# An unused early read on SyncE, and a small VectorE step placed behind a later copy

## The chip, the cores and the metric

The kernel runs on one core of a Trainium2 chip. The metric is device time in microseconds (us) of one execution, the median of several runs. Engines are named as in the profile: PE is TensorE (PEld its weight loads), DVE is VectorE, ACT is ScalarE, POOL is GpSimd, SP is SyncE.

## The reference

Two layers in a row. The first is a linear recurrence over 768 time steps for 4 batches and 8 heads of width 64, whose state decays by a constant per head; the second is a feed-forward layer over the 3072 resulting tokens of width 512, with 2048 hidden units and a "snake" activation:

```python
for t in range(S):
    state = gamma[None, :, None, None] * state + np.einsum('bhd,bhe->bhde', k[:, :, t], v[:, :, t])
    y[:, :, t] = scale * np.einsum('bhd,bhde->bhe', q[:, :, t], state)
...
h = x @ w_in
s = np.sin(alpha * h)
g = h + s * s / (alpha + 1e-09)
return (g @ w_out).astype(np.float32)
```

`alpha` has one value for each hidden unit, so `1 / (alpha + 1e-9)` is 2048 numbers: a tile `rec_alpha` of 128 partitions by 16.

## The kernel before

The recurrence is worked in chunks of 128 time steps. The 24 chunks (4 batches of 6) stand in a list `order`: the first chunk of each batch, called `e0` to `e3`, come first, since they need no state. They are grouped by 4, 2, 2, ..., 4 into the groups `g` of the feed-forward layer. For a chunk, q and k are transposed on TensorE (`half_T`, `stage_T`, copies at L292 to L307), the scores are formed (`stage_A`) and masked with the decay on VectorE (`mask_A`, tile `aT`, L345), and multiplied by v (`stage_M`, L371), whose result is copied into `xT` (L374), the input of the feed-forward layer.

A `Slot` is one step of the first feed-forward matrix: four matmuls into `ph` (L558, weights from `w_in`), the sine on ScalarE (L561, scaled by `alpha_sb`), a square on ScalarE or VectorE (`sq`, L566 or L568), and `add` on VectorE (L573), `gT = s * rec_alpha + ph`. The output matmuls with `w_out` are `ff_out` (L583, `po`); `pairs(f)` issues two of them.

The order of the instructions on every engine is written by hand: each engine works through its own list in the order of the statements and waits by semaphores for the others. The stage that the change touches is the first 25 us. There

- SyncE issues the loads `near` of q and k of chunk `e0` (L160), then `alpha_row` (L163), and nothing more until the first output at 43.8 us;
- GpSimd issues all other loads as DMAs of its own (L95, L119, L150, L154), in the order in which they are written, from the ninth on each behind the landing of the one eight places ahead of it, and works `decay_table(3)` (L254) between two of them;
- TensorE transposes `alpha_row` into PSUM (L703), ScalarE copies it to `alpha_sb` (L712), and VectorE forms `rec_alpha` from it (L728 and L729). Its first reader is the first `add`, that of slot "a";
- VectorE's list around it reads: mask of `e2`, `rec_alpha` (two instructions), copy of `stage_M(e2)` into `xT` (L374), copy of `half_T(e3, 0)` (L294), `scale_v(e2)` (L175), square of slot "a" (L568), then `add` of slots "a" and "b", the mask of `e3`, `add` of slot "c";
- `idle_work` puts matmuls on a tile of zeros between TensorE's first steps; their result is not used.

Of the kernel before, what the change touches and what calls it, by code (L numbers as in the profile page):

```python
# [8 lines left out]
F32 = mybir.dt.float32  # L9
# [7 lines left out]
def kernel(  # L17
# [15 lines left out]
    nc = tc.nc  # L33
# [22 lines left out]
    consts = ctx.enter_context(tc.tile_pool(name="consts", bufs=1))  # L56
# [9 lines left out]
    w_in_v = moe_w_in.rearrange("(ko ki) f -> ki ko f", ki=128)  # L66
# [3 lines left out]
    def half(x):  # L70
        return slice(64 * x, 64 * x + 64)
# [10 lines left out]
    def chunk_of(t, j):  # L82
        b, c = divmod(j, NCH)
        return t[b, :, c * C:(c + 1) * C, :].rearrange("h s d -> s h d")
# [12 lines left out]
    def by_rows(j, name):  # L97
        return name == "q" and j in order[1:4] or name == "k" and j in order[2:4]
# [59 lines left out]
    for name, src in (("q", q), ("k", k)):  # L158
        near[name] = work.tile([128, d_model], F32, name="o_sb", tag="o_sb", bufs=3).rearrange("i (h d) -> i h d", h=H)
        nc.sync.dma_start(out=near[name], in_=chunk_of(src, 0))  # L160
        raw[name, 0] = big.tile([128, H, D], BF16, name=f"{name}b")
    alpha_row = consts.tile([FF, 128], F32, name="alpha_row")
    nc.sync.dma_start(out=alpha_row, in_=moe_alpha.rearrange("(fo fi) -> fo fi", fi=128))  # L163

# [93 lines left out]
    alpha_sb = consts.tile([128, FF], F32, name="alpha_sb")  # L258
    rec_alpha = consts.tile([128, FF], F32, name="rec_alpha")
# [9 lines left out]
    def half_T(j, i, eng, bank=None):  # L269

        if i == 0:
            if j in order[2:4]:
                st["qkT", j] = big.tile([128, 2 * NP, 128], BF16, name="qkT0", tag="qkT0", bufs=2)
                st["kT", j] = st["qkT", j][:, NP:]
            else:
                st["qkT", j] = work.tile([128, 2 * NP, 128], BF16, name="qkT", tag="qkT", bufs=6)
        pt = psum.tile([128, NP, 128], BF16, name="pr" if by_rows(j, "qk"[i]) else "pt", tag="mm",
                       bufs=4) if bank is None else bank.rearrange("i (p t) -> i p t", p=NP)
        o = st["qkT", j][:, i * NP:(i + 1) * NP, :]
        if by_rows(j, "qk"[i]):  # L280
            for f in range(8):
                for x in range(2):
                    nc.tensor.transpose(pt.rearrange("i p t -> i (p t)")[half(x), 64 * f:64 * f + 64],
                                        raw["qk"[i], j][half(x), f, :], ident[half(x), half(x)])
            o = o.rearrange("d m (i f) -> d m i f", f=8)
            pt = pt.rearrange("d p t -> d (p t)").rearrange("d (f m i) -> d m i f", f=8, m=NP)
        else:
            for m in range(NP):
                for x in range(2):
                    nc.tensor.transpose(pt[half(x), m, :], raw["qk"[i], j][:, 4 * x + m, :], ident)  # L290
        if eng is nc.scalar:
            nc.scalar.copy(o, pt)  # L292
        else:
            nc.vector.tensor_copy(o, pt)  # L294
# [331 lines left out]
    def idle_work(n):  # L626
        for _ in range(n):
            nc.tensor.matmul(spare["ps"], warm[:, :128], warm, start=True, stop=True)  # L628
# [42 lines left out]
    def slot(name, f, lo, hi, nf=1, tag="mm"):  # L671
        sl[name] = Slot(0, f, (lo, hi), nf, tag)
# [52 lines left out]
    mask_A(e2)  # L725
    nc.scalar.activation(out=kgq, in_=expoq, func=ACTF.Exp, scale=-1.0)
    idle_work(2)
    nc.vector.tensor_scalar_add(rec_alpha, alpha_sb, 1e-9)  # L728
    nc.vector.reciprocal(rec_alpha, rec_alpha)  # L729
    nc.scalar.activation(out=tiny, in_=warm[:, 0:1], func=ACTF.Sin)  # L730
    load_chunk(order[4], "q")
    decay_table(3)
# [18 lines left out]
    stage_M(e2, front[:, 0], nc.vector)  # L751
    idle_work(1)
    half_T(e3, 0, nc.vector)
    half_T(e3, 1, nc.scalar)
    slot("a", 0, 0, n3, 1, "mm")
    scale_v(e2, nc.vector)
# [201 lines left out]
```

## Time and profile before

| | |
|---|---|
| runs | 210.97, 211.01, 212.22 us; median 211.01 |
| the profiled execution | 210.62 us, of which the span from its first to its last instruction is 208.8 |
| busy, of the span | PE 97%, DVE 75%, ACT 73%, POOL 55% |
| matmuls L558 and L583 | 98.1 and 94.8 us busy |
| first `ph` matmul | at 16.39 us |
| `rec_alpha` | add at 13.88 us for 1.62 us, reciprocal at 15.54 us for 0.25 us |
| `alpha_row` | issued on SP at 1.88 us, lands 3.8 us later |

Times in the profile are in us from the start of the span, unless a column says ns. A line of a timeline gives the start, the duration, the engine, the source line, the operation, the tiles written and read, and in brackets how long the engine stood idle before it and what ended that. The chain of waits follows the work that ended last back through whatever released it. In the DMA view a queue's line gives packets, megabytes and the share of the time of 16 DMA engines that its packets took; q1 is the queue of SyncE, q0 that of GpSimd.

### The profile page before, as it was taken

The numbers are of one execution on the slowest core, as the hardware profiler recorded it, in microseconds if no ns is written. First come the engines' busy times: TensorE is split into PE (matmuls) and PEld (weight loads), VectorE is DVE, ScalarE is ACT, GpSimd is POOL, SyncE is SP. The second block draws the span as 40 slices with busy tenths as digits, with TensorE's granted clock in tenths as the row PEclk, the third lists the DMA queues.
The fourth block names the chain that finished last, engine by engine and source line by source line (L and its number), as shares of the span: only waits on it lengthen the run. The fifth ranks groups of instructions, "written<-read, shape, count | busy, mean of one in ns | idle before, by whom it ended". The sixth has DMA issues, their size and how long they took to land.

```text
span 208.8 us, 5979 instructions
## 1 busy us (share of the span) xinstructions
PE 202.4 (97%) x2473; PEld 124.2 (59%) x2473; DVE 156.1 (75%) x322; ACT 151.5 (73%) x309; POOL 115.0 (55%) x155
## 2 busy tenths in 40 slices
PE   7798999999999999999999999999999999999994
PEld 2354544457776666666666766766767664444453
DVE  5799897797989978868878868869788965656220
ACT  7667598748997787687687687686785779999001
POOL 8996469999998989899499901002022200000000
PEclk9999999999999999999999999999999999999999
DMA  8999999999999999999999992412412101010212
GB/s 126 167 192 196 194 193 181 167 189 170 161 163 103 151 108 203 170 74 196 117 178 128 180 156 56 104 57 46 102 56 50 52 3 52 0 50 3 100 50 100
DMA packets 98187, 24.78 MB, mean 119 GB/s; under 512 B 88544, under 2 KB 95216, under 8 KB 98160
## 3 DMA queue, kind: packets, MB, share of 16 engines
q0 software_dynamic: 75408, 13.38, 85.8%
q1 hardware_dynamic: 22608, 10.96, 24.8%
q8 instruction: 19, 0.31, 0.7%
q14 instruction: 8, 0.07, 0.1%
q10 hardware_dynamic: 144, 0.07, 0.1%
HBM read 27.27 MB, written 6.29 MB: 161 GB/s over the span
## 4 chain that ended last, share of the span: by engine, by line
PE 90%; DVE 4%; DMA 2%; POOL 1%; issue 1%; ACT 0%; POOLq 0%; DVEq 0%; ACTq 0%
PE ph L558 39%; PE po L583 39%; DMA qf<-in_q_dram 2%; PE py L396 2%; DVE aT L345 2%; PE poh L608 2%; PE py L450 1%; PE pt L303 1%; PE pa L406 1%; DVE gT L573 1%; DVE rec_alpha L728 1%; PE py L459 1%; PE pa L413 1%; PE pa L435 1%; PE spare L628 1%; POOL k L119 1%
## 5 line engine op out<-in xcount | busy, mean ns | idle before, releaser
L573 DVE SCALAR_TENSOR_TENSOR gT<-s,rec_alpha,ph 128x256 bf16<-128x256 f32 (+3 forms) x164 | 79.7, 522 | 31.6 <-ACT s L566 31.4
L558 PE MATMUL ph<-xT,w_in 128*128 128x256 bf16 (+3 forms) x656 | 98.1, 291 | 0.8 <-DVE xT L374 0.8
L561 ACT ACTIVATE s<-ph,alpha_sb 128x256 f32<-128x256 f32 (+3 forms) x164 | 76.0, 506 | 30.3 <-PE ph L558 30.2
L583 PE MATMUL po<-w_out,gT 128*128 128x512 bf16 x368 | 94.8, 380 | 0.1
L558 PEld LDWEIGHTS <-w_in 128*128 128x128 bf16 x656 | 63.3, 98 | 33.7 <-issue 0.9
L566 ACT ACTIVATE s<-s 128x512 f32<-128x512 f32 (+1 forms) x91 | 56.9, 626 | 2.8
L583 PEld LDWEIGHTS <-gT 128*128 128x128 bf16 x368 | 34.0, 98 | 30.2 <-DVE gT L573 0.8
L529 POOL CAST s_q<-s_f 128x256 bf16<-128x256 f32 x5 | 2.0, 396 | 34.9 <-DVE s_f L514 18.4
L595 DVE COPY o_sb<-po 128x512 f32<-128x512 f32 x20 | 13.8, 689 | 9.9 <-PE po L583 9.8
L139 POOL DMA_DIRECT2D qk_seq<-in_q_dram x24 | 16.9, 745 | 4.0 <-DMA v_seq<-in_v_dram 3.9
L139 POOL DMA_DIRECT2D qk_seq<-in_k_dram x24 | 16.9, 748 | 1.4 <-DMA qk_seq<-in_q_dram 1.4
L139 POOL DMA_DIRECT2D v_seq<-in_v_dram x24 | 16.8, 756 | 0.0
L175 POOL TENSOR_TENSOR v_seq<-v_seq,kgq 128x512 bf16<-128x512 bf16 x13 | 13.5, 1063 | 5.1 <-DMA v_seq<-in_v_dram 5.1
L503 DVE TENSOR_TENSOR xT<-py,qg 128x512 bf16<-128x512 f32 x19 | 13.0, 682 | 0.4 <-PE py L466 0.4
L421 DVE TENSOR_TENSOR aTw<-pa,maskq 128x768 bf16<-128x768 f32 x13 | 12.3, 949 | 0.0
L119 POOL DMA_DIRECT2D vr<-in_v_dram x11 | 10.3, 944 | 0.4 <-DMA w_out<-in_moe_w_out_dram 0.3
L628 PE MATMUL spare<-warm 128*128 128x512 bf16 x24 | 8.6, 467 | 1.2 <-DVE warm L196 1.2
L612 ACT COPY o_sb<-poh 128x256 f32<-128x256 f32 (+1 forms) x2 | 0.6, 318 | 11.7 <-PE poh L608 11.2
L409 DVE TENSOR_TENSOR aT<-pa,mask 128x1024 bf16<-128x1024 f32 x7 | 8.5, 1219 | 0.0
L150 POOL DMA_DIRECT2D w_in<-in_moe_w_in_dram x7 | 5.6, 811 | 1.6 <-DMA w_out<-in_moe_w_out_dram 1.6
L529 ACT CAST s_q<-s_f 128x256 bf16<-128x256 f32 x14 | 5.5, 391 | 1.1 <-DVE s_f L525 0.6
L396 PE MATMUL py<-qkT,s_q 64*64 64x128 bf16 x160 | 6.1, 228 | 0.0
(113 smaller groups left out, 169.8 us busy)
## 6 DMA issues: line engine op xcount, KB each, us to landing
out_dram<-o_sb SPq DMA_DIRECT2D x23, 256.0 KB, 2.7
w_in<-in_moe_w_in_dram POOLq DMA_DIRECT2D x6, 256.0 KB, 11.0
w_out<-in_moe_w_out_dram POOLq DMA_DIRECT2D x3, 512.0 KB, 11.5
vr<-in_v_dram POOLq DMA_DIRECT2D x11, 128.0 KB, 6.3
qk_seq<-in_q_dram POOLq DMA_DIRECT2D x16, 80.0 KB, 6.8
qk_seq<-in_k_dram POOLq DMA_DIRECT2D x16, 80.0 KB, 5.3
v_seq<-in_v_dram POOLq DMA_DIRECT2D x16, 80.0 KB, 6.0
w_out<-in_moe_w_out_dram POOLq DMA_DIRECT2D x2, 256.0 KB, 7.1
```

What stands on the lines that cost most here:

```text
L119: nc.gpsimd.dma_start(out=t, in_=chunk_of(src, j))
L139: nc.gpsimd.dma_start(out=o, in_=src[bt, head(b, m, e), cs[0] * C:, :].rearrange("(f i) d -> i f d", i=64))
L175: eng.tensor_mul(t, t, by[:, j % NCH, :, None].to_broadcast([128, H, D]))
L421: return {"mask": lambda: nc.vector.tensor_mul(aT, pa[:, :, 0:384].rearrange("p e (m t) -> p e m t", m=2), maskq[:, None, None, :].to_broa ...
L503: nc.vector.tensor_mul(o, st["pyw", old][:, :, 0:256].rearrange("p b (m t) -> p b m t", m=2), by)
L558: nc.tensor.matmul(self.ph[:, m, :], w_in[:, i, f * 128:(f + 1) * 128], xT[g][:, i, self.lo:self.hi], start=(m == 0 and i == 0), stop=(i = ...
L561: nc.scalar.activation(out=self.s[:, m, :], in_=self.ph[:, m, :], func=ACTF.Sin, scale=alpha_sb[:, f:f + 1])
L566: nc.scalar.activation(out=self.s, in_=self.s, func=ACTF.Square)
L573: nc.vector.scalar_tensor_tensor(gT[self.g][:, f, self.lo:self.hi], self.s[:, m, :], rec_alpha[:, f:f + 1], self.ph[:, m, :], op0=ALU.mult ...
L583: nc.tensor.matmul(po[g, ts], gT[g][:, f, ts * C:(ts + 1) * C], w_out[:, f, :], start=(f == 0), stop=(f == FF - 1))
L595: nc.vector.tensor_copy(o_sb, po[g, ts])
L628: nc.tensor.matmul(spare["ps"], warm[:, :128], warm, start=True, stop=True)
```

## The change

It has two parts. After the `near` loads, SyncE issues one more DMA, which reads 32 rows of 256 float32 (1 KB each) of `w_in` into a tile `wake` that nothing reads; `alpha_row` follows it. And the two instructions of `rec_alpha` are issued behind VectorE's copy of `half_T(e3, 0)`, instead of ahead of the copy of `stage_M(e2)`.

```diff
@@ -159,6 +159,8 @@
         nc.sync.dma_start(out=near[name], in_=chunk_of(src, 0))
         raw[name, 0] = big.tile([128, H, D], BF16, name=f"{name}b")
+    wake = consts.tile([32, 256], F32, name="wake")
+    nc.sync.dma_start(out=wake, in_=w_in_v[0:32, 0, 0:256])
     alpha_row = consts.tile([FF, 128], F32, name="alpha_row")
@@ -725,8 +727,6 @@
     idle_work(2)
-    nc.vector.tensor_scalar_add(rec_alpha, alpha_sb, 1e-9)
-    nc.vector.reciprocal(rec_alpha, rec_alpha)
     nc.scalar.activation(out=tiny, in_=warm[:, 0:1], func=ACTF.Sin)
@@ -751,6 +751,8 @@
     stage_M(e2, front[:, 0], nc.vector)
     idle_work(1)
     half_T(e3, 0, nc.vector)
+    nc.vector.tensor_scalar_add(rec_alpha, alpha_sb, 1e-9)
+    nc.vector.reciprocal(rec_alpha, rec_alpha)
     half_T(e3, 1, nc.scalar)
```

No other instruction changes its place on any engine.

## The prediction

> **What bounds the kernel now.** I read the page first, then the chain of waits from 7 to 24 us, then the timeline of VectorE and GpSimd there, then the DMA view. The page (first line: span; then busy time and chain by engine):
>
> ```profile
> span 208.8 us, 5979 instructions
> PE 202.4 (97%) x2473; PEld 124.2 (59%) x2473; DVE 156.1 (75%) x322; ACT 151.5 (73%) x309; POOL 115.0 (55%) x155
> PE 90%; DVE 4%; DMA 2%; POOL 1%; issue 1%; ACT 0%; POOLq 0%; DVEq 0%; ACTq 0%
> ```
>
> TensorE is 90% of the chain. From 22 us on it is busy nearly without a break, so whatever is won must be won before it, by starting that row of matmuls earlier. The chain of waits there (start, length, what):
>
> ```profile
> 3.09 4.83 DMA qf<-in_q_dram
> 7.97 0.44 PE pr L283 x16
> ...
> 12.75 1.22 DVE aT L345
> 13.97 1.55 DVE rec_alpha L728
> ...
> 15.71 0.64 DVE xT L374
> ...
> 16.39 0.82 PE ph L558 x4
> ...
> 19.67 1.13 DVE aT L345
> 20.80 0.53 DVE gT L573
> ...
> 21.38 0.82 PE po L583 x3
> ```
>
> Both places of the change lie near it. `rec_alpha`'s add stands on it for 1.55 us, ahead of the copy `xT` (L374) for which the first `ph` matmul waits 0.78 us. The load `qf` stands on it because `pr` waits 0.38 us for it; the new read runs just before that.
>
> **Why the add takes 1.62 us.** It handles 16 numbers per partition. The timeline (start, length, engine, line):
>
> ```profile
> 13.88 1.62 DVE L728 TENSOR_SCALAR rec_alpha<-alpha_sb 128x16 f32<-128x16 f32 x1
> 14.32 1.14 POOL L254 TENSOR_TENSOR qg<-qg,step 128x512 f32<-128x512 f32 x1
> 15.32 0.85 POOL L150 DMA_DIRECT2D w_in<-in_moe_w_in_dram  x1
> 16.12 0.79 POOL L150 DMA_DIRECT2D w_in<-in_moe_w_in_dram  x1
> 16.25 0.68 DVE L294 COPY qkT<-pr 128x512 bf16<-128x512 bf16 x1
> 17.91 0.56 DVE L568 TENSOR_TENSOR s<-s 128x384 f32<-128x384 f32 x1 [0.39 <-ACT s L561]
> ```
>
> It ends at 15.50, GpSimd's multiply at 15.46. So it looks held until GpSimd is done, after which it needs about 0.04 us. Two casts from and to SBUF show the same against GpSimd's DMA issues:
>
> ```profile
> 3.98 0.56 DVE L689 CAST qb<-o_sb 128x512 bf16<-128x512 f32 x1 [0.28 <-DMA o_sb<-in_q_dram]
> 4.24 0.63 POOL L95 DMA_DIRECT2D qf<-in_q_dram  x1
> 5.29 0.75 DVE L693 CAST kb<-o_sb 128x512 bf16<-128x512 f32 x1 [0.75 <-DMA o_sb<-in_k_dram]
> 5.73 0.95 POOL L119 DMA_DIRECT2D vr<-in_v_dram  x1
> ```
>
> They end at 4.54 and 6.04, 0.30 and 0.31 us after one issue gives way to the next, although their lengths differ by 0.19 us. So a held cast gets in where one DMA issue follows another. The Trainium skill, SBUF — State Buffer, section Who interferes with whom, says that GpSimd and a VectorE copy or scalar operation of this kind share a port pair by an exclusive lock, held for a whole instruction; by that rule, the trace agrees (15.50 against 15.46).
>
> **The move, step by step.** Removed at its old place: 1.55 us of chain for the add, and 0.25 us from 15.46 to the start of `xT` at 15.71 for its end and the reciprocal. Without them `xT` waits only for its matmuls (L371, 14.25 to 14.66): about 14.71 to 15.35. The copy of `half_T(e3,0)` needs `pr`, which ends at 15.36: 15.40 to 16.08. Nothing else moves on VectorE. TensorE issues the second `pr` group until 15.61 in any case, so the first `ph` starts at 15.61 instead of 16.39: at most 0.78 us is won. ScalarE is free for the first sine (its table load ends 15.55, its copy of `pr` 16.25): 16.53 instead of 17.30.
>
> Added at the new place: the same two instructions, between that copy and `scale_v(e2)` (L175, 0.68 us), which stands ahead of the first square (L568). Instructions on VectorE start some 0.09 us before the previous one's end, so the add asks at about 15.99. GpSimd has no gap from 1.38 to 16.91, so its hours do not move with VectorE: its first `w_in` issue gives way at 16.12, its second ends at 16.91, and then it waits for a landing until 17.70. Two outcomes:
> - It gets in at 16.12: `scale_v` starts 0.25 us later, 16.37, ends 17.05, before the sine ends (17.12). The square starts at 17.14 instead of 17.91. The whole 0.77 us remains.
> - It misses and is held to 16.91: `scale_v` 17.16 to 17.84, square at about 17.8 instead of 17.91. About 0.1 us remains, as everything behind (gT, the mask `aT` of e3, gT, then `po`) is a row of VectorE work.
>
> So the move is worth 0.1 to 0.77 us. What waits behind the add if it is held: `scale_v(e2)`, the square, and TensorE's `po`, which had next to no spare time (0.27 us of waiting at 21.38).
>
> **The read `wake`, step by step.** 32 KB on SyncE between the `near` loads and `alpha_row`. Nothing reads it, so no engine waits for it. SyncE: one issue more (L160 0.57 us, L163 0.82), so `alpha_row` is issued at about 2.5 to 2.7 instead of 1.88 and lands, at its 3.8 us, near 6.5; its transpose runs at 8.68, so 2 us cover it. SyncE's next work is at 43.8 us. The DMA engines: packets of 1 KB show in the stretch 6.0 to 6.4 us:
>
> ```profile
> DMA packets 70, 0.07 MB, mean 179 GB/s; under 512 B 0, under 2 KB 70, under 8 KB 70
> q0 software_dynamic: 70, 0.07, 112.7%
> ```
>
> That is 1.127 x 16 x 0.4 us / 70 = 0.103 us of an engine each. Two per engine, if the 32 spread evenly over 16, are 0.21 us, or 0.18 at the 1.13 packets that overlap. The engines are full then, so `qf` lands between 0 and 0.2 us later; I take 0.1, as they need not run ahead of the packets of `qf`. The Trainium skill, DMA: Bandwidth & Descriptors, section Queues, rings and completion order, lets each engine take turns between its queues packet by packet; by that rule the read does delay `qf`, and the sum would be its upper end, 0.2; no row here separates these. The delay moves VectorE's row from 8 us on, and with it the add's request: 15.99 + 0.1 = 16.09, just ahead of 16.12; at 0.2 it is 16.19, and the gap is missed.
>
> **What is given back.** Landings do not come earlier. `w_in`'s second piece is issued at 9.57 and lands 7.8 us later, 17.37, used at 18.11; the piece for slot 8 is issued at 15.32, lands 11.6 later, 26.92, and its weights are loaded at 27.48. Spare time is 0.74 and 0.56 us, less the 0.1 by which the read puts loads off. So of 0.77 - 0.1 = 0.67 us TensorE keeps about 0.45. Later landings have over 1 us (w_out's last, 28.56 + 10.5 = 39.06, used 40.10).
>
> **Sum.** -0.67 + 0.22 = -0.45 us. The profiled execution took 210.62 us, span 208.8 and 1.8 around it; the runs' median is 211.01, 0.4 above, for the same program. Against the median: 210.6. That is 0.2%; a measurement of this kernel tells about 1% from no change.
>
> **Rivals.**
> 1. The stall moves. The add misses the gap and waits to 16.91: gain 0.1, 210.9 us. For it: the request and the gap lie 0.03 us apart in my sum. Against: the two casts each got in at the next gap.
> 2. Slower: the 1.55 us are the instruction's own (its first use, or its source), not GpSimd's. Then the add runs 15.99 to 17.61, `scale_v` 17.86 to 18.54, the square at 18.46 instead of 17.91: +0.55, 211.6 us. It decides as soon as the add ends after 17.1 at its new place. For it: L207, another small one of these, took 0.54 us. Against: that one too ends (2.45) where a GpSimd issue ends (2.48), and the agreement at 15.46.
> 3. The read costs more. Its bound: `o_sb` of k, 1024 packets, landed in 4.0 us, 64 per engine, 0.06 us for 256 B, so up to 0.25 for 1 KB and 0.5 for two. Even so, held to 16.91, the gain is 0.1 to 0; 211.0 us.
> 4. The read helps the loads behind it. In 1.6 to 2.4 us the engines moved 232 packets, in 2.4 to 3.2 already 864: a slow start. If it shortened `qf`'s 4.83 us, `pr` could come 0.38 earlier: with the move 0.38 + 0.77 = 1.15 us, 209.9. Against: those first packets are the `near` loads, which the read follows.
> 5. The change does nothing: another wait (the second `pr` group, sine, landings) holds TensorE at today's hours: 211.0 us.
>
> **Chances.** Forecast 0.38, rival 1 0.22, rival 2 0.12, rival 3 0.05, rival 4 0.08, rival 5 0.05; 0.10 for what no row shows. All worked-out cases lie within 1% of 211.01 (208.9 to 213.1). The three runs themselves differ by 0.6%, and the starting state of the loads can move an early stage more than I see; this puts 0.16 below and 0.12 above, 0.72 within. Range 209.4 to 212.0: from rival 4 less the runs' own scatter to rival 2 plus it.
>
> **What would show it.** Right: the add at its new place under 0.3 us, ending by 16.2; first `ph` near 15.7; the square near 17.2; `po` (three) near 20.8 instead of 21.38. Stall moved: the add ends at about 16.95. Rival 2: 1.6 us there whatever GpSimd does. For the read: `qf` lands after 7.92, `alpha_row` stays off the chain. Wrong altogether: TensorE waiting for a landing before 30 us by over 0.5 us, or a span beyond 207.3 to 210.

## The result, and the profile after

| | before | after |
|---|---|---|
| median of the runs made side by side | 211.88 us (20 runs) | 210.61 us (20 runs) |
| profiled execution, and its span | 210.62, 208.8 us | 210.65, 208.9 us |

The ratio is 0.9964 with a 95% interval of 0.9946 to 0.9981, so the change makes the kernel faster by 0.36%, or 0.76 us (0.40 to 1.14). The comparison leaves disturbed executions out, so this is not the ratio of the two medians. The two profiled executions are equal, and the profile shows why. The page of after:

```profile
span 208.9 us, 5981 instructions
PE 202.3 (97%) x2473; PEld 124.1 (59%) x2473; DVE 154.4 (74%) x322; ACT 151.6 (73%) x309; POOL 115.1 (55%) x155
PE 92%; DMA 3%; DVE 2%; POOL 1%; issue 0%; ACT 0%; POOLq 0%; ACTq 0%
```

VectorE is busy 1.7 us less, and its share of the chain fell from 4% to 2%. Lines from L163 on carry higher numbers than before: L558 is now L560, the add is L754. The chain of waits of after (start, length, what):

```profile
3.09 5.76 DMA qf<-in_q_dram
8.90 0.44 PE pr L285 x16
...
15.92 0.62 PE pr L285 x32
16.54 0.77 PE ph L560 x4
...
18.01 0.57 DVE s L570
...
21.48 0.82 PE po L585 x3
```

`rec_alpha` has left the chain: the first `ph` now follows TensorE's own second `pr` group. But `qf` took 5.76 us instead of 4.83, so `pr` starts 0.93 us later than before (8.90 against 7.97). At `ph` the lag is 0.15 us by the chain and at `po` 0.10: this execution lost 0.93 us at a landing and won it back behind it. The timeline of VectorE and GpSimd in after shows the add at its new place:

```profile
16.94 0.20 DVE L754 TENSOR_SCALAR rec_alpha<-alpha_sb 128x16 f32<-128x16 f32 x1
16.35 1.55 POOL L150 DMA_DIRECT2D w_in<-in_moe_w_in_dram  x2
17.15 0.75 POOL L150 DMA_DIRECT2D w_in<-in_moe_w_in_dram  x1
```

The second POOL line is the second of the two issues in the line above it. The add takes 0.20 us instead of 1.62 and ends at 17.14, where one issue gives way to the next: the same gap that the prediction aimed at, 1.03 us later. GpSimd's row came later too, 0.46 us of it in a wait for a landing of `w_in` ahead of 13.54 us that before did not have.

For the experiments I read one more number from each trace: by how much a certain matmul starts later than the same matmul of the profiled before. It is called the lag, at `pr` (8.05 us in before), at a `ph` at 19.26, at a `po` at 37.35 and at the last `poh` at 205.60. For after it is +0.93, +0.10, +0.10, +0.10.

### The profile page after: what moved, and what is told of

Same layout as the page of the kernel before. It is cut to its first block, busy times and chain, and to the rows that moved or that the text cites. A ratio compares the mean times of both kernels' runs of the same rounds, so it can differ in the third digit from the quotient of the medians.

```text
span 208.9 us, 5981 instructions
## 1 busy us (share of the span) xinstructions
PE 202.3 (97%) x2473; PEld 124.1 (59%) x2473; DVE 154.4 (74%) x322; ACT 151.6 (73%) x309; POOL 115.1 (55%) x155
## 4 chain that ended last, share of the span: by engine, by line
PE 92%; DMA 3%; DVE 2%; POOL 1%; issue 0%; ACT 0%; POOLq 0%; ACTq 0%
PE ph L560 39%; PE po L585 39%; DMA qf<-in_q_dram 3%; PE py L398 2%; PE poh L610 2%; PE py L452 1%; PE spare L630 1%; DVE aT L347 1%; PE pt L305 1%; PE pa L408 1%; DVE gT L575 1%; PE py L461 1%; PE pa L415 1%; PE pa L437 1%; PE front L373 1%; POOL k L119 1%
## 5 line engine op out<-in xcount | busy, mean ns | idle before, releaser
L560 PE MATMUL ph<-xT,w_in 128*128 128x256 bf16 (+3 forms) x656 | 98.1, 291 | 0.0
L560 PEld LDWEIGHTS <-w_in 128*128 128x128 bf16 x656 | 63.2, 98 | 33.0 <-issue 0.2
L347 DVE TENSOR_TENSOR aT<-pa,dec 128x1024 bf16<-128x1024 f32 x4 | 4.9, 1219 | 1.8 <-PE pa L335 1.8
```

The costliest lines, as they stand in the source:

```text
L560: nc.tensor.matmul(self.ph[:, m, :], w_in[:, i, f * 128:(f + 1) * 128], xT[g][:, i, self.lo:self.hi], start=(m == 0 and i == 0), stop=(i = ...
```

## The experiments

Each run was timed beside the kernel before on its own chip; ratios are to that kernel, in brackets the 95% interval.

### The two parts, alone and together

`neither` is the kernel before once more and `both` the changed kernel once more. `move` has only this:

```diff
-    nc.vector.tensor_scalar_add(rec_alpha, alpha_sb, 1e-9)
-    nc.vector.reciprocal(rec_alpha, rec_alpha)
...
     half_T(e3, 0, nc.vector)
+    nc.vector.tensor_scalar_add(rec_alpha, alpha_sb, 1e-9)
+    nc.vector.reciprocal(rec_alpha, rec_alpha)
```

and `read` only this:

```diff
+    wake = consts.tile([32, 256], F32, name="wake")
+    nc.sync.dma_start(out=wake, in_=w_in_v[0:32, 0, 0:256])
```

> The kernel before once more, as a measure of how far its own front varies. Both theories: ratio 1.000 within 0.002. If the 0.93 us by which qf landed later in the changed kernel's profile (8.85 us against 7.92) is a matter of the execution, qf lands here somewhere between 7.9 and 8.9; if the read causes it, it lands near 7.9 again. The rec_alpha add takes about 1.6 us at its old place.

> rec_alpha at its new place, no read. Theory A (the move pays, the read costs): 0.5 to 0.8 us faster than before, ratio 0.9962 to 0.9976, at least as fast as both parts together; the add takes 0.2 to 0.3 us at its new place, qf lands near 7.9. Theory B (the read pays by making the start steadier, the move is neutral): ratio 0.999 to 1.001.

> The read of w_in, rec_alpha at its old place. Theory A: 0.1 to 0.9 us slower than before, ratio 1.0005 to 1.004, and the rec_alpha add again held about 1.6 us until GpSimd's multiply ends; qf lands later than 7.92. Theory B: ratio near 0.9964 as with both parts, with fewer runs near 212 us.

> The changed kernel once more, on the same chip as its two halves. Both theories: ratio about 0.996. If the late qf landing belongs to the read, it lands near 8.85 again; if to the execution, anywhere between 7.9 and 8.9.

| | ratio | median us | lag at pr, ph, po, end | the add |
|---|---|---|---|---|
| neither | 1.0014 [0.9978, 1.0050] | 211.82 | +1.14, +0.69, +1.74, +1.74 | 0.71 us |
| move | 0.9964 [0.9922, 1.0005] | 210.97 | +0.41, -0.42, -0.01, -0.02 | 0.19 us |
| read | 1.0024 [0.9980, 1.0068] | 211.77 | +0.14, +0.14, +0.30, +0.29 | 1.61 us |
| both | 0.9988 [0.9941, 1.0034] | 211.14 | +0.61, -0.21, +1.23, +1.30 | 0.17 us |

What follows. The move alone comes out at the 0.9964 of the whole change, though its own interval just reaches past 1; the read alone gives no gain. The changed kernel once more, `both`, comes out at 0.9988, with 0.9964 inside its interval. From `pr` to `ph`, after, move and both each win 0.83 us, to the hundredth, whatever their `pr` lost; read, with the add at the old place, wins nothing there. `neither` shows the lottery in the old place: its front ran later (the `near` load of k took 4.80 us instead of 4.0, and the lag is 1.52 from 8.8 us on), GpSimd's list had come further when the add asked, and the add was held 0.71 instead of 1.62 us; its lag also falls by 0.83, to 0.69. So 0.83 us is all that can be won there, because TensorE's second `pr` group then sets the first `ph`; the move makes sure of it.

Behind `ph`, however, `neither` loses 1.05 us, `both` 1.44 and `move` 0.41, by 37 us. The groups of the trace put it on single squares of VectorE. The timeline of both:

```profile
28.05 2.18 DVE L570 TENSOR_TENSOR s<-s 128x512 f32<-128x512 f32 x1
28.61 1.06 POOL L256 TENSOR_TENSOR qg<-qg,step 128x512 f32<-128x512 f32 x1
```

A square of this size takes 0.68 us at 26.66, just ahead of it; this one takes 2.18 and ends at 30.23, 0.56 us after GpSimd's multiply ends (29.67). In neither one took 1.78 us at 28.95; in move one took 1.58 us at 32.00 and also ended 0.56 us after a multiply. In before the four squares between 26 and 35 us take 0.68 to 0.85 us; the longest also ends 0.56 us after a multiply, which it met only at its tail. The multiplies are `decay_table(1)`, `(4)` and `(2)`, which stand behind DMA issues that wait for landings, so that their hours shift from execution to execution and meet a square or don't. The next runs take this away.

### Another source for the add, and earlier tables

`psum` leaves the add at its old place but lets it read the PSUM tile `pal`, from which ScalarE copies `alpha_sb`:

```diff
-    nc.vector.tensor_scalar_add(rec_alpha, alpha_sb, 1e-9)
+    nc.vector.tensor_scalar_add(rec_alpha, pal, 1e-9)
```

`tables` works the three decay tables right behind `load_w_out(2)`, at 18.5 to 21.5 us, between VectorE's first square (17.2 us) and its next (26.2 us):

```diff
     load_w_out(2)
+    for c in (1, 4, 2):
+        decay_table(c)
...
-    decay_table(1)
...
-    decay_table(4)
...
-    decay_table(2)
```

`move_tables` and `psum_tables` join the latter to `move` and to `psum`. None of the four has the read.

> rec_alpha at its old place and no read, but the add takes alpha from the transpose's PSUM tile instead of alpha_sb. If GpSimd holds the add because it takes both operands' sides from SBUF (theory H), the add takes 0.2 us at about 14.0 and xT follows when its matmuls are done, so the row behind it comes as early as with the move (0.8 us earlier than with the add held), ratio 0.9955 to 0.998. If the wait belongs to the place or to the instruction itself (rival), it stays near 1.6 us and the ratio at 1.000.

> The kernel before with the three later decay tables (1, 4, 2) multiplied on GpSimd right behind load_w_out(2), at about 18.5 to 21.7 us, instead of among the loads at 29 to 35 us. Theory H: the five 128x512 squares on VectorE from 26 us on take 0.7 us each in any execution (1.33 to 2.18 where they met a table before), the lag that the front has at 22 us is the lag of the whole span, ratio 0.995 to 0.999. Rival (TensorE waits there for weights that land late, as the prediction's give-back had it): TensorE still loses 0.2 to 1 us between 28 and 36 us, ratio 1.000 or above, since the loads behind the tables are issued later.

> The move without the read, and the three tables early as in the run before. Theory H: the 0.8 us of the move stay to the end, with no loss between 28 and 36 us: 1.0 to 1.4 us faster than before, ratio 0.993 to 0.995. Rival: no better than the move alone, 0.996 to 1.000.

> The add from PSUM at its old place and the three tables early. Theory H: as the move with early tables or 0.1 us better, since the add and the reciprocal then lie in VectorE's wait for the matmuls of e2: ratio 0.992 to 0.995. Rival: 0.998 to 1.002.

| | ratio | median us | lag at pr, ph, po, end | the add |
|---|---|---|---|---|
| psum | 0.9948 [0.9914, 0.9982] | 210.77 | +0.66, -0.17, +0.24, +0.53 | 0.17 us |
| tables | 0.9960 [0.9916, 1.0003] | 212.41 | +0.10, -0.73, -0.72, -0.09 | 0.17 us |
| move_tables | 0.9922 [0.9890, 0.9954] | 210.49 | -0.01, -0.84, -0.84, -0.49 | 0.29 us |
| psum_tables | 0.9905 [0.9871, 0.9940] | 210.42 | +0.40, -0.38, -0.32, -0.21 | 0.17 us |

The timeline of psum:

```profile
14.67 0.17 DVE L728 TENSOR_SCALAR rec_alpha<-front 128x16 f32<-128x16 f32 x1
14.11 0.88 POOL L119 DMA_DIRECT2D qkr<-in_q_dram  x1
15.01 1.05 POOL L254 TENSOR_TENSOR qg<-qg,step 128x512 f32<-128x512 f32 x1
```

The add runs at the old place in 0.17 us, while GpSimd is in a DMA issue (14.11 to 14.99), and 0.83 us are won between `pr` and `ph` as by the move. The add of before asked, at 13.88 us, inside the issue of the same load (timeline of before):

```profile
13.43 0.97 POOL L119 DMA_DIRECT2D qkr<-in_q_dram  x1
```

From SBUF it was held through the rest of that issue and the multiply behind it; from PSUM it ran inside the issue at once, and so it did in the five later runs with this source (0.17 us each, always inside a DMA issue). None of the six ran beside a multiply. The 1.62 us were thus not the instruction's own. In tables the add, still from SBUF and at the old place, also took 0.17 us, at 13.99, just ahead of the end of an issue (14.17); so this run differs from before in two things, and its ratio can't be put on the tables alone. In move_tables the squares stay at their own length (timeline):

```profile
31.57 0.69 DVE L568 TENSOR_TENSOR s<-s 128x512 f32<-128x512 f32 x1 [0.85 <-ACT s L561]
18.02 3.04 POOL L254 TENSOR_TENSOR qg<-qg,step 128x512 f32<-128x512 f32 x3
```

In all three kernels with early tables no later square of VectorE is held, and from `ph` to `po` TensorE loses at most 0.06 us. By the traces, the squares were what gave back time in `both` and `move`; the ratios of move and move_tables have intervals that overlap.

A third place shows at the end of the rows: psum, tables and move_tables lose 0.29 to 0.63 us between 37 us and the end. At 62 us the two scalar operations of `later_mask` (L243) take 1.01, 1.27 and 1.07 us there, instead of 0.68 in before, beside GpSimd's DMA issues, and TensorE loses 0.29, 0.55 and 0.35 us at 69 us. It loses nothing there, to 0.02 us, in the runs in which the pair takes up to 0.73 us, and 0.04 and 0.08 at 0.76 and 0.80 (psum_tables and both). quiet_read and quiet_read4 below don't fit: they lose 0.33 and 0.68 us there at 0.70 and 0.58.

### The read on a quieter kernel, and the mask moved too

`quiet` is psum_tables again. `quiet_read` adds the read of the change to it, and `quiet_read4` one of 128 packets:

```diff
+    wake = consts.tile([128, 256], F32, name="wake")
+    nc.sync.dma_start(out=wake, in_=w_in_v[:, 0, 0:256])
```

`quiet_mask` moves `later_mask` to where GpSimd's issues don't meet it:

```diff
+    later_mask()
     sl["t"].add()
...
-    at((2, 0), lambda: later_mask())
```

> The add from PSUM with the early tables once more, as the base for the three others. Theory H (GpSimd holds VectorE at three places of the kernel before): 1.3 to 2.2 us faster than before, ratio 0.990 to 0.994; TensorE's lag behind the kernel before at 22 us is the lag at its end, to 0.3 us.

> The same with the read of 32 packets of 1 KB. If the read is priced as in the prediction (0 to 0.2 us by which qf lands later): slower than the base by 0 to 0.2 us, ratio against before up to 0.001 above the base's. If the read itself caused the 0.93 us of late landing in the changed kernel's profile: 0.6 to 1 us slower than the base, 0.003 to 0.005 above.

> The same with four times the read, 128 packets of 1 KB (the first 256 columns of 128 rows of w_in). By the prediction's 0.2 us of each engine for 32 packets: qf lands 0.4 to 0.8 us later, 0.4 to 0.8 us slower than the base. If the DMA engines had room there: no difference to the base.

> The base with later_mask (two scalar operations and a copy on VectorE) taken from the second group, where it lies beside GpSimd's DMA issues at 62 us, to a wait of VectorE ahead of slot t's add at 24 us. Theory H: the pair of scalar operations takes 0.3 to 1.2 us there too, inside or just behind VectorE's wait of 0.5 us; TensorE loses nothing at 68 us (it lost 0.29 to 0.65 us there where the pair took 1.0 to 1.3): 0 to 0.4 us faster than the base. If it is held at 24 us for a whole DMA issue: up to 0.6 us slower than the base.

| | ratio | median us | lag at pr, ph, po, end |
|---|---|---|---|
| quiet | 0.9936 [0.9896, 0.9977] | 210.53 | +0.04, -0.78, -0.66, -0.40 |
| quiet_read | 0.9995 [0.9945, 1.0045] | 213.26 | +1.27, +1.89, +4.03, +4.36 |
| quiet_read4 | 0.9961 [0.9922, 1.0001] | 214.80 | +1.10, +0.27, +4.90, +6.76 |
| quiet_mask | 0.9910 [0.9874, 0.9946] | 210.33 | +0.05, -0.78, -0.71, -0.60 |

The read is not settled by these. With it, three comparisons out of three come out slower (read 1.0024 against neither 1.0014, both 0.9988 against move 0.9964, quiet_read 0.9995 against quiet 0.9936), each within its intervals; and four times the packets come out at 0.9961, not four times as dear: that is 0.25% or 0.5 us above quiet, where 0.4 to 0.8 was expected. The medians show what these ratios don't: 3 of the 12 executions of quiet took over 213 us, 7 of quiet_read and 7 of quiet_read4. Whether the read makes such executions more frequent is not shown; in the first comparison after, with the read, had 2 of 20 and before 5 of 20. In the profiles `pr` lags by 0.74 us on average in the four with 32 packets (0.14 to 1.27) and by 0.31 in the nine without (-0.01 to 1.14). The scatter among kernels with the same loads is wider than the difference.

The profiles of quiet_read and quiet_read4 are of two of these long executions (214.90 and 217.31 us). They show what a late `qf` can be followed by, not what the read costs. In quiet_read TensorE waited 1.59 us for it. Two stretches of that trace (window; time; busy time and count of PE, PEld, DVE, ACT, POOL; granted clock; DMA share; GB/s):

```profile
9.00:10.00 1.00, 0.76 (x22) 0.70 (x24) 0.31 (x1) 0.14 (x1) 0.56 (x2) 0.67 2.44 157
10.00:13.00 3.00, 3.00 (x22) 1.20 (x18) 0.03 (x1) 1.95 (x9) 2.99 (x5) 0.54 1.85 175
```

The granted clock is 0.67 and then 0.54 on average in these stretches, and 1.00 from 13 us on; the four spare matmuls take 1.82 us instead of 0.97, and the lag grows from 1.27 to 2.72 us by 15 us. Behind the waits of 1.13 us (after) and 1.26 us (quiet_read4) for `qf` the clock stayed at 1.00. In quiet_read4 the early tables met the first square instead of a later one (timeline):

```profile
18.18 4.00 DVE L570 TENSOR_TENSOR s<-s 128x384 f32<-128x384 f32 x1 [0.39 <-ACT s L563]
18.72 3.04 POOL L256 TENSOR_TENSOR qg<-qg,step 128x512 f32<-128x512 f32 x3
```

Three multiplies in a row held it for 4.00 instead of 0.56 us, and TensorE idled 3.03 us ahead of a `po`; its granted clock was then 0.50 from 24.2 to 27.5 us. So the early tables are no cure for a late front; they change who is hit.

quiet_mask has the lowest median and a ratio of 0.9910 [0.9874, 0.9946], where the change itself has 0.9964 [0.9946, 0.9981]. The two were not timed beside each other, and these intervals meet at 0.9946. Nor can the quieter versions be ranked: psum_tables has 0.9905, and quiet, the same kernel again, 0.9936. The two scalar operations of the mask take 0.59 us there, at 23.46.

What the mask alone adds to quiet (0.9936) can't be told from nothing by the times. Its trace shows no loss at 69 us, but that of quiet, with the mask at its old place, shows none there either, so this run does not test the third place.

## Why the prediction was right, and where it was not

The forecast was 210.6 us, a gain of 0.45 us or 0.2%; measured are 0.36% (0.19 to 0.54%), or 0.76 us, and a median of 210.61. That the median meets the forecast to a hundredth is luck: the forecast was counted from 211.01, and beside the changed kernel the kernel before had 211.88. By its steps:

- *Why the add takes 1.62 us*: right. It takes 0.17 to 0.29 us wherever GpSimd gives way or the operand is in PSUM, and 0.71 in neither, where 0.66 us of the multiply were left. By the Trainium skill, SBUF — State Buffer, section Who interferes with whom, a scalar operation of this kind can contend with GpSimd in the mode in which it also uses the port pair that they share; the trace agrees as to the stall, 1.62 us from SBUF beside a GpSimd multiply against 0.17 from PSUM inside the same issue of GpSimd in which the other was first held. That the tile in PSUM keeps it out of that mode was not shown by itself. Rival 2, the instruction's own 1.55 us, is out.
- *The move*: right in outcome and nearly in size, 0.83 instead of 0.77 us. All four executions with the add at the new place got in (0.17 to 0.29 us), so rival 1, the stall that moves, did not happen. They asked 0.05 to 0.30 us ahead of the next issue, where the forecast had 0.03; but GpSimd's hours did not stand still as it assumed, and that issue began at 16.30 to 17.15 instead of 16.12. That both rows shifted by about as much was not foreseen. The other hours need an on-time `qf`. With it, and the add at its new place, move_tables has the first `ph` at 15.54 (forecast 15.61), the add at 16.00 (15.99), the square at 17.07 (17.14) and `po` at 20.54 (near 20.8); in after all of them come with the 0.93 us of the late `qf`. What I had missed: the 0.83 us are lost only when the old add is held for the whole of GpSimd's multiply, which happened in two of the four profiles with that add in SBUF and at that place (before and read; in neither it was held for the multiply's tail, in tables not at all, and no `ph` waited for it). The profile of before was one of the dear executions; how many of the timed ones were is not known.
- *The read*: open. 0.1 us was forecast, and rival 3 allowed 0.5; the three pairs differ by 0.10, 0.24 and 0.59%, which is 0.2, 0.5 and 1.2 us, with intervals of about 0.4% on each side of each ratio. Rival 4, that it helps the loads, has nothing for it. `alpha_row` stayed off the chain, as said.
- *What is given back, 0.22 us*: the wrong mechanism for nearly all of it. The prediction had TensorE wait for pieces of `w_in` that land too late. In after, move and both its weight loads wait for none. In psum, psum_tables, quiet and quiet_mask they do, 0.21 to 0.41 us, at about 27 us, where the prediction had counted the spare time (timeline of quiet):

```profile
27.00 0.98 PEld L558 LDWEIGHTS <-w_in 128*128 128x128 bf16 x6 [0.31 <-DMA w_in<-in_moe_w_in_dram]
```

But the matmuls lose 0.09 us by it in psum_tables and nothing in the others. What gives time back, when it does, is VectorE's squares held behind GpSimd's decay tables at 28 to 36 us. By the lag from `ph` to `po` that is 0 in after, 0.16 in read, 0.41 in move and psum, 1.05 in neither, 1.44 in both, and at most 0.12 in the kernels with the tables out of the way and `qf` within 0.4 us of before. What I had worked out for the add I had not worked out for the squares, which in the profiled before take 0.68 to 0.85 us and so looked free of it. That 0.22 us lies among these losses is luck.
- *Rival 5*, nothing won because something else holds TensorE: out for the median (the interval stays below 1), though in single executions the lost time at `qf` hides all of the gain, as in the two profiles of before and after.

## What to carry to other kernels

Where a small VectorE instruction lasts many times its size's worth, look at what GpSimd ends at that instant, and then at every other two-input or copy-like VectorE instruction that GpSimd's list can meet; moving one takes away one meeting only. Reading the operand from PSUM took the stall away without any new order. And when the first loads of a kernel scatter by 1 us, compare a late matmul's lag with the lag at the first landing: a profile each of before and after shows the sum of both, here zero.

## What had not been expected of the hardware

- A square that reads its operand twice from SBUF is held by GpSimd's multiply, not only copies and scalar operations: 1.34 to 2.18 us instead of 0.69, and 4.00 instead of 0.56 when three multiplies follow each other without a break; in that one execution it did not get in between them, whereas the adds got in where one DMA issue followed another. The squares at 34 us in before, after, move, read and psum began inside a DMA issue ahead of a multiply and took only 0.79 to 0.87 us, ending 0.25 us after the issue; that of `both` at 28.05 began inside one too and was held through the multiply. What decides between the two is open.
- The first loads land at different times in kernels whose loads are the same: the `near` load of k took 4.80 us in neither and 4.0 in before, and the `pr` that waits for `qf` starts 0.66 us later in psum than in before.
- In quiet_read a wait of 1.59 us near the start was followed by a granted clock of 0.50 for about 3.4 us, while waits of 1.13 us (after) and 1.26 us (quiet_read4) there, and one of 1.75 us at 23.2 us in quiet_read, were not. In quiet_read4 the same fall came behind the wait of 3.03 us. Each fall was seen once, and what decides is open.
- In `neither` the first matmuls ran slowly for longer (eight transposes in 0.64 us at 9.63, in before 0.41 at 8.34). The view of stretches gives a granted clock of 1.00 there, but the trace holds no clock record ahead of 10.14 us, where the pace changes; the first record, of full clock, stands at 4.81 us in before and at 6.96 in move. The Trainium skill, TensorE: Matmul & The Clock Gate, section Part 1: The HAM clock gate, lets the time of the clock's rise vary between executions, since the window that watches TensorE does not start with the kernel; the three executions agree that it varies.
